# Moving every large SBUF tile of an attention and two-layer MLP kernel to a multiple of 2 KB

## The chip, the cores and the metric

The kernel runs on one core of a Trainium2 chip. Its engines are named as the profile names them: PE is the matrix engine (PEld its weight loads), DVE the vector engine, ACT the scalar engine, POOL the GpSimd engine, SP the engine whose queue issues the DMAs. The metric is the device time of one execution in microseconds (us). On-chip memory here means SBUF: 128 partitions, and each tile has the same byte address in all of them.

## What is computed

```python
# attention: 2 x 8 heads, 768 positions, head size 64
scores = q @ k.T / 8 + bias          # bias = -slope(head) * distance
a = softmax(where(keep, scores, -1e9))   # keep: 8 global keys and the 96 last ones
x = (a @ v).reshape(1536, 512)
# layer 1, d_ff 2048
h = x @ w_in;  x = softplus(h) @ w_out
# layer 2, d_ff 2048
h = x @ w_in;  x = (h * clip(h + 3, 0, 6) / 6) @ w_out
```

## The kernel before

`body` (L763) opens one pool of small constants, `const`, and calls `fast_path` (L411). `fast_path` opens the pool `xp` with the transposed activations (`xsh`, `xsl`: the high and the low part of x, three tiles each of 8 KB a partition) and builds `Layers` (L52), which opens `mp` (the split activations `gh` and `gl`), `tp` (scratch `t`), `pp` (three 8 KB tiles `part` of partial sums, and the one-column constant `three` that the second layer's ACT instruction at L182 adds), `wp0` (six slots of four 2 KB weight tiles `w`) and `wr0` (raw weights and their scratch `wa`). After these `fast_path` opens the pools of attention: `ap_r`, `ap2` (`qT`), `ap_v` (`V`), `ap_m` (`pm` and the row statistics), `ap_t` (`pT`) and `ap1` (`kT`, `gk`, `zeros`, `bias`). When attention is over, its pools close and `wp1` and `wr1` take their place: five more slots of weights.

A bump allocator lays the pools one behind the other in the order in which they are opened; a tile takes its size, rounded up to 32 bytes. No table says where a tile begins: it is the sum of all that was opened earlier.

Every product of the layers is written as three products of float32r parts (high by low, low by high, high by high; `matmul3`, L188), all issued at L193. Each of them is one LDWEIGHTS of 128 columns and one MATMUL. The moving operand is streamed through the array, the stationary one is loaded ahead of it. Which tile is which differs by stage:

| stage | output | moving operand (columns) | stationary operand (128 columns) |
|---|---|---|---|
| first layer, first phase, beside attention | `hf`, `accf` | `xsh`/`xsl`, `gh`/`gl` (256) | `w` |
| first layer, rest | `h`, `acc` | `xsh`/`xsl`, `gh`/`gl` (512) | `w` |
| second layer | `h`, `acc` | `xsh`/`xsl` for `h`, `w` for `acc` (512) | `w` for `h`, `gh`/`gl` for `acc` |
| closing stage (`last_items`, L302) | `hz`, `accz` | `xsh`/`xsl` for `hz`, `w` for `accz` (512, the last block in halves of 256) | `w` for `hz`, `g` for `accz` |

The closing stage keeps its `gh` and `gl` for all five chunks at once, so `last_items` puts them not into `mp` but into free weight slots of `wp0` and `wp1` (`where`, L316, tiles named `g`). Everything else about `accz` is as in the second layer's `acc`.

The raw weights are float64, read as pairs of 32-bit words, and are turned into the two float32r parts of `w` on the chip (`unit_convert`, L117: ACT L133 and L145, POOL L136, DVE L137, L140, L141, L146), one or two units beside each item of matmuls. While attention runs, the first raw tiles and scratch tiles are parts of `part` instead of `wr0`. In the last phases `check_step` (L611) reads q and k once more, squares them on ACT (L624) and sets a flag that decides whether a second, general path is run; with these inputs it is not.

The engines each take their instructions in the order written out at build time by a scheduler; waits are on semaphores.

Of the kernel before, what the change touches and what calls it, by code (L numbers as in the profile page):

```python
# [7 lines left out]
F32 = mybir.dt.float32  # L8
# [8 lines left out]
P = 128  # L17
# [20 lines left out]
BIG = float(2 ** 38)  # L38
FAR = 1.0e9
SCALE = 0.125  # L40
EPS = 1e-9
SQ_LIMIT = 1.0e9
W_LO = 2.0 ** -15
# [8 lines left out]
class Layers:  # L52
# [3 lines left out]

    def __init__(self, ctx, tc, weights, xsh, xsl, out):
        self.ctx, self.tc, self.nc = ctx, tc, tc.nc  # L60
        self.weights, self.xsh, self.xsl, self.out = weights, xsh, xsl, out
        self.pool("mp", 2)
        self.pool("tp", 5)
        self.pool("pp", 1)
        self.part = [self.pp.tile([P, 4, GB], F32, name=f"part{g}") for g in range(T // GB)]
        self.three = self.pp.tile([P, 1], F32, name="three")
        self.nc.vector.memset(self.three, 3.0)
        self.W, self.raws, self.slot = {}, {}, {}
        self.done, self.loaded = 0, 0
        first = range(PHASES[0][0])  # L70
        early = range(2 * EARLY_PAIRS)
        self.order = [(j, u) for js in (early, first[len(early):]) for u in range(2) for j in js]
        self.order += [(j, u) for j in range(len(first), 2 * NCH) for u in range(2)]
        self.free, self.h_tags, self.acc_tags, self.wr = [], [], [], []
        self.room = None
        self.n_h, self.halves, self.in_first, self.beside = 0, 0, True, False
        self.grow(0, FIRST_SLOTS, 2, 2)
# [318 lines left out]
def x_tiles(ctx, tc):  # L396
    xp = ctx.enter_context(tc.tile_pool(name="xp", bufs=1))
    return tuple(
        [xp.tile([P, KC, GB], F32R, name=f"xs{z}{g}") for g in range(T // GB)] for z in "hl"
    )  # L400


def softmax_rows(nc, sm, rs, pm):

    nc.vector.tensor_scalar(out=rs, in0=sm, scalar1=EPS, scalar2=None, op0=ALU.add)
    nc.vector.reciprocal(out=rs, in_=rs)  # L406
# [1 line left out]
        nc.gpsimd.tensor_scalar(out=t, in0=t, scalar1=rs[:, j:j + 1], scalar2=0.0, op0=ALU.mult, op1=ALU.add)  # L408


def fast_path(tc, ident, nf, counts, q, k, qt, kt, v, weights, out, flag):  # L411


    with ExitStack() as ctx, ExitStack() as actx:
        nc = tc.nc
        xsh, xsl = x_tiles(ctx, tc)
        layers = Layers(ctx, tc, weights, xsh, xsl, out)
        layers.beside = True
        tp = layers.tp
        layers.room = actx.enter_context(tc.tile_pool(name="ap_r", bufs=1))  # L420
# [52 lines left out]
        for h in range(H):  # L473
            nc.scalar.mul(bias[:, h, 2, :], far[:, 2, :], -SLOPES[h] / SCALE)

        def bias_of(hs):
            for h in hs:
                tc.keep_in_program_order(nc.vector.tensor_scalar(
                    out=bias[:, h, 0:2, :], in0=far[:, 0:2, :], scalar1=-SLOPES[h] / SCALE, scalar2=None, op0=ALU.mult
                ))  # L480
# [6 lines left out]
        def att_s(k):  # L487
# [28 lines left out]
            for z in range(4):  # L516
# [3 lines left out]
                    in1=bias[:, 4 * e + z, mo:mo + nsl, :].rearrange("p s t -> p (s t)"),  # L520
                    scale=-SCALE, scalar=3.0e38, op0=ALU.add, op1=ALU.min, accum_out=nm[:, z:z + 1],
                )
# [138 lines left out]
def dense_attention(tc, ident, nf, q, k, v, xsh, xsl):  # L661

    with ExitStack() as ctx:
# [25 lines left out]
        for i in range(NB):  # L689
# [20 lines left out]
            for b in range(B):  # L710
                for c in range(KC):
# [8 lines left out]
                    for j in range(2):  # L720
# [4 lines left out]
                        for z in range(2):  # L725
# [3 lines left out]
                            )  # L729
                            nc.scalar.mul(pm[:, z * S // 2:(z + 1) * S // 2], ps[:, z, 0:S // 2], SCALE)  # L730
                        nc.vector.scalar_tensor_tensor(
# [19 lines left out]
                    nc.vector.tensor_tensor(out=xl, in0=px, in1=r32(xh), op=ALU.subtract)  # L751


def general_path(tc, ident, nf, q, k, v, weights, out):
    with ExitStack() as ctx:
        xsh, xsl = x_tiles(ctx, tc)
        dense_attention(tc, ident, nf, q, k, v, xsh, xsl)
        layers = Layers(ctx, tc, weights, xsh, xsl, out)
        layers.weight_step(2 * FIRST_SLOTS)
        layers.run()  # L760


def body(tc, q, k, v, qt, kt, ns, w1i, w1o, w2i, w2o, out):  # L763
    nc = tc.nc
    with ExitStack() as ctx:
        nc.scalar.preload_act_table_set("natural_log_exp_and_others")
        const = ctx.enter_context(tc.tile_pool(name="const", bufs=1))
        ident = const.tile([P, P], F32, name="ident")

        nsb = const.tile([P, 2, 2], I32, name="nsb")  # L770
        nc.sync.dma_start(out=nsb.rearrange("p n w -> p (n w)"), in_=ns.partition_broadcast(P))
        nf = const.tile([P, 2], F32, name="nf")
        cv = const.tile([P, 2, 2], F32, name="cv")
        cneg = const.tile([P, 2], F32, name="cneg")

        def counts():
            tc.keep_in_program_order(nc.vector.tensor_copy(cv, nsb))
            nc.vector.tensor_scalar(out=cneg, in0=cv[:, :, 0], scalar1=0.0, scalar2=None, op0=ALU.is_lt)
            nc.vector.tensor_tensor(out=cneg, in0=cneg, in1=cv[:, :, 1], op=ALU.add)
            nc.vector.scalar_tensor_tensor(  # L780
                out=nf, in0=cneg, scalar=float(2 ** 32), in1=cv[:, :, 0], op0=ALU.mult, op1=ALU.add
            )

        make_identity(nc, ident)
        flag = const.tile([1, 1], I32, name="flag")
        weights = (w1i, w1o, w2i, w2o)
        fast_path(tc, ident, nf, counts, q, k, qt, kt, v, weights, out, flag)
        redo = nc.values_load(flag[0:1, 0:1], min_val=0, max_val=1)
        with tc.If(redo > 0):
            general_path(tc, ident, nf, q, k, v, weights, out)  # L790


def layout(q, k, v, n_global, n_local, moe_w_in, moe_w_out, moe2_w_in, moe2_w_out):
# [43 lines left out]
```

## Time and profile before

| | us |
|---|---|
| median of 3 runs (range) | 643.96 (643.88 to 644.82) |
| the profiled execution | 643.55 |
| its span, first to last instruction | 641.8 |
| PE busy in it | 622.3 |
| DVE busy | 425.7 |
| ACT busy | 380.8 |
| POOL busy | 148.1 |

The profiled execution is 0.41 us under the median, and 1.75 us of it lie outside the span. Busy time of PE counts a matmul from its start to a modelled end, so that neighbours overlap; what a matmul costs in a stream is the step from one start to the next. The chain that ended last goes back from the last instruction to what released each one; where PE works without a gap, a piece of it is a number of matmuls and the time that they took together, which gives the step.

### The profile page before, as it was taken

To read this page: it belongs to the slowest core of one execution; us is meant where nothing else is said; L and a number is where in the kernel's file an instruction comes from. 1 tells how busy PE (TensorE), PEld (TensorE's weight loads), DVE (VectorE), ACT (ScalarE), POOL (GpSimd) and SP (SyncE) were. 2 spreads that over 40 slices of the span, in tenths; PEclk is the share of its full clock that TensorE was granted. 3 is DMA by queue.
4 is the path that set the end of the run, shared out by engine and by line. 5 is a ranking of instruction groups with operands and counts; after the bars stand their busy time and mean duration, and the time that the engine had idled before them with its cause. 6 is when DMAs were issued, how large, how long until landed. Compare 5 with 4: busy or idle time off the path is not lost.

```text
span 641.8 us, 9651 instructions
## 1 busy us (share of the span) xinstructions
PE 622.3 (97%) x3496; PEld 513.1 (80%) x3496; DVE 425.7 (66%) x893; ACT 380.8 (59%) x808; POOL 148.1 (23%) x180
## 2 busy tenths in 40 slices
PE   8699999999999999999999999999999999999996
PEld 4477987899999888887888888888887888888785
DVE  6988687735799999999989994126723342424251
ACT  7978888764868877696777652326694222222230
POOL 4666354330133255352200600001000000000000
PEclk9989999999999999999999999999999999999999
DMA  8754231101233333433402132001562000001011
GB/s 279 247 172 137 72 100 38 42 5 66 73 126 133 130 115 118 131 130 100 132 1 66 66 106 91 0 1 33 164 197 67 0 1 0 2 1 65 1 67 70
DMA packets 25081, 53.67 MB, mean 84 GB/s; under 512 B 2496, under 2 KB 9152, under 8 KB 25024
## 3 DMA queue, kind: packets, MB, share of 16 engines
q1 hardware_dynamic: 25024, 52.96, 25.4%
q8 instruction: 29, 0.48, 0.3%
q14 instruction: 28, 0.23, 0.1%
HBM read 49.81 MB, written 3.15 MB: 83 GB/s over the span
## 4 chain that ended last, share of the span: by engine, by line
PE 62%; DVE 17%; ACT 9%; DMA 5%; issue 3%; POOL 3%; SPq 0%; ACTq 0%; POOLq 0%; DVEq 0%
PE acc L193 21%; PE h L193 21%; PE accf L193 6%; PE hf L193 5%; ACT pm L523 3%; DVE wa L140 2%; DMA chk<-in_q 2%; PE accz L193 2%; PE hz L193 2%; DVE wa L141 2%; DVE w L146 2%; PE ptp L546 2%; POOL wa L136 1%; ACT chk L624 1%; PE px L564 1%
## 5 line engine op out<-in xcount | busy, mean ns | idle before, releaser
L193 PE MATMUL h<-xsh,w 128*128 128x512 f32 x584 | 159.1, 396 | 0.0
L136 POOL TENSOR_SCALAR wa<-wa 128x512 f32<-128x512 f32 x56 | 79.4, 1423 | 235.4 <-ACT wa L133 235.2
L193 PEld LDWEIGHTS h<-xsh,w 128*128 128x128 f32 x584 | 109.3, 188 | 26.7 <-DVE t L179 0.7
L193 PE MATMUL acc<-w,gh 128*128 128x512 f32 x344 | 108.0, 395 | 0.0
L183 DVE SCALAR_TENSOR_TENSOR t<-t,h 128x512 f32<-128x512 f32 x43 | 29.4, 684 | 82.3 <-ACT t L182 82.3
L193 PE MATMUL h<-xsl,w 128*128 128x512 f32 x292 | 82.3, 395 | 0.0
L182 ACT ACTIVATE t<-h,three 128x512 f32<-128x512 f32 x43 | 29.5, 687 | 87.7 <-PE h L193 87.5
L185 DVE TENSOR_TENSOR gl<-t,gh 128x512 fp32r<-128x512 f32 x73 | 51.3, 703 | 42.9 <-ACT gh L184 42.6
L193 PE MATMUL acc<-gh,w 128*128 128x512 f32 x240 | 78.9, 396 | 0.3 <-DVE part L289 0.2
L193 PEld LDWEIGHTS acc<-w,gh 128*128 128x128 f32 x344 | 64.5, 188 | 15.7
L184 ACT CAST gh<-t 128x512 fp32r<-128x512 f32 x73 | 45.2, 619 | 46.3 <-PE acc L193 24.3
L193 PE MATMUL acc<-w,gl 128*128 128x512 f32 x172 | 68.2, 396 | 0.1
L408 POOL TENSOR_SCALAR pm<-pm,rs 128x256 f32<-128x256 f32 (+1 forms) x96 | 54.4, 585 | 58.9 <-DVE rs L406 34.2
L193 PEld LDWEIGHTS h<-xsl,w 128*128 128x128 f32 x292 | 54.8, 188 | 13.2
L193 PE MATMUL accf<-ghf,w 128*128 128x256 f32 x288 | 56.6, 286 | 0.2 <-ACT ghf L184 0.2
L193 PEld LDWEIGHTS acc<-gh,w 128*128 128x128 f32 x240 | 44.9, 188 | 11.9 <-DVE part L289 0.6
L523 ACT ACTIVATE pm<-pm,nm 128x256 f32<-128x256 f32 (+1 forms) x96 | 46.3, 485 | 3.3 <-DVE nm L518 3.1
L193 PE MATMUL acc<-gl,w 128*128 128x512 f32 x120 | 47.5, 396 | 0.0
L193 PE MATMUL hf<-xsh,w 128*128 128x256 f32 x288 | 47.2, 289 | 0.0
L193 PEld LDWEIGHTS accf<-ghf,w 128*128 128x128 f32 x288 | 45.9, 188 | 0.6 <-ACT ghf L184 0.4
L146 DVE TENSOR_TENSOR w<-wa,w 128x512 fp32r<-128x512 f32 x56 | 39.4, 705 | 8.9 <-ACT w L145 8.9
L145 ACT CAST w<-wa 128x512 fp32r<-128x512 f32 x56 | 34.3, 615 | 14.4 <-DVE wa L141 8.9
(115 smaller groups left out, 1045.9 us busy)
## 6 DMA issues: line engine op xcount, KB each, us to landing
raw<-in_w2i SPq DMA_DIRECT2D x16, 512.0 KB, 3.3
raw<-in_w2o SPq DMA_DIRECT2D x16, 512.0 KB, 3.3
raw<-in_w1i SPq DMA_DIRECT2D x14, 512.0 KB, 3.4
raw<-in_w1o SPq DMA_DIRECT2D x12, 512.0 KB, 3.3
V<-in_v SPq DMA_DIRECT2D x12, 256.0 KB, 3.0
chk<-in_q SPq DMA_DIRECT2D x12, 256.0 KB, 3.0
chk<-in_k SPq DMA_DIRECT2D x12, 256.0 KB, 2.8
qT<-in_qt SPq DMA_DIRECT2D x11, 256.0 KB, 3.9
```

Of the source, the lines that this page charges most:

```text
L136: nc.gpsimd.tensor_scalar(out=a, in0=a, scalar1=W_HI, scalar2=W_LO, op0=ALU.min, op1=ALU.max)
L140: nc.vector.scalar_tensor_tensor(out=ai, in0=hi, scalar=-2 ** 30, in1=ai, op0=ALU.bitwise_and, op1=ALU.bitwise_or)
L141: nc.vector.scalar_tensor_tensor(out=ai, in0=lo, scalar=29, in1=ai, op0=ALU.logical_shift_right, op1=ALU.bitwise_or)
L145: nc.scalar.copy(wh, a)
L146: nc.vector.tensor_tensor(out=wl, in0=a, in1=r32(wh), op=ALU.subtract)
L182: nc.scalar.activation(t1, hf, AF.Relu, bias=self.three[:, 0:1])
L183: nc.vector.scalar_tensor_tensor(out=t3, in0=t1, scalar=6.0, in1=hf, op0=ALU.min, op1=ALU.mult)
L184: nc.scalar.copy(gh, t3)
L185: nc.vector.tensor_tensor(out=gl, in0=t3, in1=r32(gh), op=ALU.subtract)
L193: return self.nc.tensor.matmul(out, lhsT=a, rhs=b, start=start and z == 0, stop=stop and z == len(seq) - 1, **kw)
L408: nc.gpsimd.tensor_scalar(out=t, in0=t, scalar1=rs[:, j:j + 1], scalar2=0.0, op0=ALU.mult, op1=ALU.add)
L523: nc.scalar.activation(pmz, pmz, AF.Exp, bias=nm[:, z:z + 1], scale=-1.0, accum_out=sm[:, z:z + 1])
```

## The change

The constant `three` moves from `pp` into `const`, and takes 1,248 bytes there (312 float32 columns, of which the first is used) instead of 32. Its memset is now issued in `body`; it stays the first instruction of DVE. In the path that runs, the order of all instructions on all engines, their shapes and their waits are those of before; what differs is the addresses.

```diff
+EDGE = 312
...
-    def __init__(self, ctx, tc, weights, xsh, xsl, out):
+    def __init__(self, ctx, tc, weights, three, xsh, xsl, out):
...
-        self.three = self.pp.tile([P, 1], F32, name="three")
-        self.nc.vector.memset(self.three, 3.0)
+        self.three = three
...
         make_identity(nc, ident)
         flag = const.tile([1, 1], I32, name="flag")
+        three = const.tile([P, EDGE], F32, name="three")[:, 0:1]
+        nc.vector.memset(three, 3.0)
```

Where the tiles begin, as the built programs have it (first byte of the pool, and in brackets what it is past a multiple of 2,048):

| pool | tiles | before | after |
|---|---|---|---|
| `xp` | `xsh`, `xsl` | 17,184 (800) | 18,432 (0) |
| `mp` | `gh`, `gl` | 66,336 (800) | 67,584 (0) |
| `tp` | `t`, `rel`, `far` and the like | 74,528 (800) | 75,776 (0) |
| `pp` | `part` | 84,768 (800) | 86,016 (0) |
| `wp0` | `w`, and `g` in the closing stage | 109,376 (832) | 110,592 (0) |
| `wr0` | `raw`, `wa` | 158,528 (832) | 159,744 (0) |
| `ap_r`, `ap2`, `ap_v`, `ap_m` | raw, `qT`, `V`, `pm` | 170,816 (832) | 172,032 (0) |
| `ap_t` | `pT` | 203,968 (1,216) | 205,184 (384) |
| `ap1` | `kT`, then `gk`, `zeros`, `bias` | 212,160 (1,216) | 213,376 (384) |
| `wp1` | `w`, and `g` in the closing stage | 170,816 (832) | 172,032 (0) |
| `wr1` | `raw`, `wa` | 211,776 (832) | 212,992 (0) |

The row statistics in `ap_m` (12 tiles of 32 bytes) stand ahead of `ap_t`, so `pT`, `kT` and what follows begin 384 bytes past. Before, the pools up to `pp` stood 32 bytes off those behind it, because of the 32 bytes of `three`; after, both groups stand at the same offset. The identity used by the transposes stays at 16,512 (128).

## Rows read from the trace of the kernel before

**Rows 1.** Page, the span and the busy time by engine.
```profile
span 641.8 us, 9651 instructions
...
PE 622.3 (97%) x3496; PEld 513.1 (80%) x3496; DVE 425.7 (66%) x893; ACT 380.8 (59%) x808; POOL 148.1 (23%) x180
```
**Rows 2.** Chain that ended last, shares of the span by engine, then by line.
```profile
PE 62%; DVE 17%; ACT 9%; DMA 5%; issue 3%; POOL 3%; SPq 0%; ACTq 0%; POOLq 0%; DVEq 0%
by line: PE acc L193 21.5%; PE h L193 20.7%; PE accf L193 6.3%; PE hf L193 5.3%; ACT pm L523 2.9%; issue 2.8%; DVE wa L140 2.2%; DMA chk<-in_q 2.2%; PE accz L193 2.2%; PE hz L193 2.2%; DVE wa L141 2.1%; DVE w L146 1.8%; PE ptp L546 1.8%; PO
```
**Rows 3.** Chain in order of time, second layer: start us, us, what.
```profile
508.76 2.80 PE acc L193 x12
511.56 2.80 PE h L193 x12
514.36 2.80 PE acc L193 x12
```
**Rows 4.** The same, end of the first layer's first phase.
```profile
168.74 2.84 PE hf L193 x24
171.59 2.84 PE accf L193 x24
174.42 2.84 PE hf L193 x24
```
**Rows 5.** The same, the closing stage.
```profile
612.17 9.32 PE hz L193 x40
621.49 12.03 PE accz L193 x60
```
**Rows 6.** The same, asked for 623 to 630 us alone.
```profile
622.88 7.25 PE accz L193 x32
```
**Rows 7.** Timeline of PE, the last block's halves: start us, us, operation, names.
```profile
631.67 1.72 PE L193 MATMUL accz<-w,g 128*128 128x256 f32 x13
```
**Rows 8.** PE by line and shape: busy us, mean ns of one, idle before.
```profile
L193 PE MATMUL accf<-glf,w 128*128 128x256 f32 x144 | 40.5, 282 | 0.9 <-DVE glf L185 0.9
L193 PE MATMUL hf<-xsl,w 128*128 128x256 f32 x144 | 22.9, 281 | 0.0
```
**Rows 9.** Windows: busy us of PE, PEld, DVE, ACT, POOL, PEclk, DMA share, GB/s.
```profile
211.00:301.00 90.00, 89.82 (x385) 71.81 (x383) 89.49 (x154) 66.86 (x117) 39.81 (x22) 1.00 0.37 122
441.00:490.00 49.00, 49.00 (x211) 39.31 (x210) 25.63 (x42) 34.42 (x83) 3.48 (x5) 1.00 0.51 151
505.00:525.00 20.00, 20.00 (x88) 16.07 (x87) 4.83 (x7) 4.68 (x8) 0.00 (x0) 1.00 0.00 1
623.00:630.00 7.00, 7.00 (x33) 5.79 (x32) 0.98 (x3) 0.62 (x1) 0.00 (x0) 1.00 0.01 2
```
**Rows 10.** Chain in order of time, around 301 and 490 us.
```profile
300.78 0.63 ACT gh L184
301.41 0.04 issue
301.45 0.73 PE acc L193 x2
...
486.08 2.59 DMA chk<-in_k
...
489.48 0.52 ACT gh L184
490.00 0.02 issue
490.02 0.70 DVE gl L185
```
**Rows 11.** One line each of ACT and DVE: ns min/median/max, first and last start.
```profile
L145 ACT CAST w<-wa x56: 602/613/627, 35.4 to 471.1; 128x512 fp32r<-128x512 f32 x56
L145 ACT CAST w<-part x8: 614/625/653, 21.5 to 91.1; 128x512 fp32r<-128x512 f32 x8
...
L146 DVE TENSOR_TENSOR w<-wa,w x56: 673/680/1080, 37.2 to 471.7; 128x512 fp32r<-128x512 f32 x56
L146 DVE TENSOR_TENSOR w<-part,w x8: 654/680/944, 22.8 to 92.3; 128x512 fp32r<-128x512 f32 x8
```
**Rows 12.** DMA issues: KB each, median us from issue to landing.
```profile
chk<-in_q SPq DMA_DIRECT2D x12, 256.0 KB, 3.0
chk<-in_k SPq DMA_DIRECT2D x12, 256.0 KB, 2.8
```
**Rows 13.** The memset of `three`: ns min/median/max, first and last start.
```profile
L67 DVE MEMSET three<- x1: 59/59/59, 0.8 to 0.8; 128x1 f32 x1
```
**Rows 14.** Timeline of PE, the second warm-up on tile `zeros`, bf16.
```profile
9.44 1.47 PE L647 MATMUL warm<-zeros 128*128 128x512 bf16 x6
```
**Rows 15.** The warm-up's line: ns min/median/max, first and last start.
```profile
L647 PE MATMUL warm<-zeros x24: 379/384/634, 1.2 to 17.6; 128*128 128x512 bf16 x24
```

More of the change, by code (lines that the diff above doesn't have):

```diff
@@ L408, in softmax_rows, with fast_path @@
         nc.gpsimd.tensor_scalar(out=t, in0=t, scalar1=rs[:, j:j + 1], scalar2=0.0, op0=ALU.mult, op1=ALU.add)
-def fast_path(tc, ident, nf, counts, q, k, qt, kt, v, weights, out, flag):
+def fast_path(tc, ident, three, nf, counts, q, k, qt, kt, v, weights, out, flag):
     with ExitStack() as ctx, ExitStack() as actx:
@@ L416, in fast_path @@
         xsh, xsl = x_tiles(ctx, tc)
-        layers = Layers(ctx, tc, weights, xsh, xsl, out)
+        layers = Layers(ctx, tc, weights, three, xsh, xsl, out)
         layers.beside = True
@@ L751, in dense_attention, with general_path @@
                     nc.vector.tensor_tensor(out=xl, in0=px, in1=r32(xh), op=ALU.subtract)
-def general_path(tc, ident, nf, q, k, v, weights, out):
+def general_path(tc, ident, three, nf, q, k, v, weights, out):
     with ExitStack() as ctx:
@@ L757, in general_path @@
         dense_attention(tc, ident, nf, q, k, v, xsh, xsl)
-        layers = Layers(ctx, tc, weights, xsh, xsl, out)
+        layers = Layers(ctx, tc, weights, three, xsh, xsl, out)
         layers.weight_step(2 * FIRST_SLOTS)
@@ L785, in body @@
         flag = const.tile([1, 1], I32, name="flag")
+        three = const.tile([P, EDGE], F32, name="three")[:, 0:1]
+        nc.vector.memset(three, 3.0)
         weights = (w1i, w1o, w2i, w2o)
-        fast_path(tc, ident, nf, counts, q, k, qt, kt, v, weights, out, flag)
+        fast_path(tc, ident, three, nf, counts, q, k, qt, kt, v, weights, out, flag)
         redo = nc.values_load(flag[0:1, 0:1], min_val=0, max_val=1)
         with tc.If(redo > 0):
-            general_path(tc, ident, nf, q, k, v, weights, out)
+            general_path(tc, ident, three, nf, q, k, v, weights, out)
 def layout(q, k, v, n_global, n_local, moe_w_in, moe_w_out, moe2_w_in, moe2_w_out):
```

## The prediction

> **What bounds the kernel now.** I read the busy times first, then the chain that ended last, then single stretches of that chain. PE is busy in 97% of the span and no other engine in more than 66% [rows 1]. The chain shows where that matters: 62% of it lies on PE, the rest on DVE, ACT, DMA and POOL, and its largest pieces are the matmuls of L193: `acc` 21.5%, `h` 20.7%, `accf` 6.3%, `hf` 5.3%, `accz` and `hz` 2.2% each [rows 2]. The change leaves every instruction as it was and moves operands, so the question is whether the step from one matmul to the next depends on where its operands lie. Such a dependence would show as different steps for equal shapes.
>
> They differ. In the second layer 12 matmuls of 512 columns take 2.80 us, both for `acc` and for `h`: a step of 233.3 ns [rows 3]. In the first phase, 24 of 256 columns take 2.84 us: 118.3 ns [rows 4]. In the closing stage `hz` still has 9.32 / 40 = 233.0 ns, and `accz`, right behind it, is quicker: 12.03 us for 60, of which 15 have half the columns [rows 5]. The part of it without halves and without its first matmuls has 7.25 / 32 = 226.6 ns [rows 6]. So the same shape has two steps, 6.7 ns apart. The halves of the last block go the other way: 13 of them end 1.72 us after the first starts; less the modelled length of one, some 0.28 us [rows 8], that is 1.44 / 12 = 120.0 ns [rows 7], 1.7 ns more than a 256-column matmul has elsewhere.
>
> What sets `accz` apart? [...] Not the shape or the order of products, which are those of `acc`. By the table of addresses it is this: everywhere else in the layers one operand begins 800 bytes past a multiple of 2 KB (`xp` or `mp`) and the other, a weight tile, 832; in `accz` both are weight slots, at 832. A difference of 32 bytes between the operands, or one operand off a multiple of 64 bytes, goes with 233.3 ns; equal offsets on multiples of 64 go with 226.6 ns. Whether the odd operand is the moving one (`h`) or the stationary one (`acc` of the second layer) makes no difference [rows 3]. Straddling a 2 KB boundary is not it: `hf` at 168.74 us reads x from byte 800 of a 2 KB row on, `hf` at 174.42 us from 1,824 on and over the boundary, and both take 2.84 us [rows 4]. After the change every operand of L193 begins at a multiple of 512 bytes, and all are alike.
>
> **The change, part by part.** *Matmuls of 512 columns.* `acc`, `h` and `hz` hold 21.5 + 20.7 + 2.2 = 44.4% of the chain [rows 2], 285 us of 641.8, or 1,221 steps of 233.3 ns. At 226.6 ns each saves 6.7 ns: 8.2 us off the path.
>
> *Matmuls of 256 columns.* `accf` and `hf` hold 11.6%, 74.4 us or 629 steps of 118.3 ns. At the 120.0 ns of the closing halves they cost 1.1 us more. I take this in full, since it is the only row with equal offsets; the other end is nothing.
>
> *Stretches where PE is not the chain.* From 211 to 301 us DVE is busy 89.49 of 90 us, and from 441 to 490 the chain runs through the reloads of q and k and their squares on ACT; PE works 385 and 211 matmuls there [rows 9]. A shorter step gains nothing in them: PE comes to the same `gh` and `gl` earlier and waits. At 301.45 it starts 0.04 us behind the ACT cast of `gh`, at 490 it waits for `gl`, queued on DVE behind a cast that stood behind a square on ACT, which waited for its DMA [rows 10]. What is late next is thus known: 385 x 6.7 ns = 2.6 us of new idle time on PE before 301 us, 211 x 6.7 ns = 1.4 us before 490. If those engines yielded it after all, 4.0 us more would be gained; if PE followed DVE up to 345 us, some 189 more steps or 1.3 us would be lost.
>
> *ACT and DVE.* The weight cast on ACT takes 613 ns from `wa` (832 to 832) and 625 ns from `part` (800 to 832); the DVE difference behind it takes 680 ns in both cases [rows 11]. DVE gains nothing by this; on ACT 12 of 625 ns of its 9% (58 us) [rows 2] would be at most 1.1 us. I take 0, as nearly all of ACT's work has one offset already.
>
> *DMA.* It holds 5% of the chain, 32 us [rows 2]. No row shows a landing on a 2 KB multiple; the reloads of q and of k, equal in size and place, differ by 0.2 of 3.0 us [rows 12], so I allow 7% either way, 2.2 us, and take 0. [...]
>
> *The constant.* The memset takes 59 ns at 0.8 us [rows 13] and stays DVE's first instruction: 0.
>
> The sum is -8.2 + 1.1 = -7.1 us. The profiled execution has 643.55 us, 0.41 less than the median; off that median, 643.96, it gives 636.9 us. Its own range is 632 (the 4.0 us yielded and something of ACT or DMA) to 640.4 (1.3 and 2.2 us lost).
>
> **The rivals.** *Addresses do not matter.* Then `accz` is quicker for a reason that I do not see, for instance because only there do both operands lie above byte 109,376. For it: its first six matmuls are slower than the rest (12.03 us less 15 x 0.12 and 39 x 0.2266 leaves 1.39 us, 232 ns each [rows 5]), although their operands lie at 832 as well. Against it: no matmul of 512 columns outside it shows the short step in the rows I read, at any distance of the operands. Time: 644.0, or 645.1 if the 256-column matmuls alone take their 120.0 ns. [...]
>
> *Equal places collide: slower.* The moving tile and the first slice of the weights would now begin at the same place of a 2 KB row in nearly every matmul, on a multiple that no row shows, and the loading of the next weights beside the stream could hold the stream up. The halves at 120.0 against 118.3 ns [rows 4, 7] show that equal offsets can cost. Priced at as large a step the other way, 6.7 ns on 1,221 matmuls and 1.1 us on the short ones: 653.3 us. It decides as soon as the step of `h` passes 234.4 ns (1.3 us over 1,221).
>
> *Finer alignment gives more.* 832 is a multiple of 64 and of no larger power of two, so `accz` may not be the best. The bf16 warm-up has six matmuls of 512 columns in 1.47 us [rows 14], less the length of one, 0.38 [rows 15]: 218 ns. At that step 1,221 x 15.3 ns = 18.7 us would go: 625.3 us. Nothing shows that float32r reaches it.
>
> **How the numbers follow.** A measurement of this kernel can tell about 0.2%, 1.3 us, from no change. The forecast gets 0.58: the contrast is clean, but rests on one stage and its cause on a table. No effect gets 0.22, slower 0.12, more gain 0.08. Faster by over 0.2%: the forecast and the larger gain less a little for a gain eaten by waits, 0.64; within: 0.22; slower: 0.14, with the case of 645.1. The range runs from the forecast's low end, 632, to the no-effect case with its 1.1 us, 645.1; outside are the larger gain and most of the collision, under 0.2.
>
> **What would show it.** Right: 12 `h` or `acc` in 2.72 us instead of 2.80, `hz` at the step of `accz`, `hf` and `accf` 24 in 2.88, `accz` unchanged, PE idle some 2.6 us before 301 us and a chain there on DVE as now. Wrong: `h` still 2.80 per 12 (addresses do not matter), over 2.81 (collision), or near 2.62 (finer alignment). If the step falls and the time does not, the gain sits as idle time on PE in front of `gh` and `gl`.

## The result, and the profile after

| | before | after |
|---|---|---|
| median of 4 runs (range), us | 643.98 (643.88 to 644.82) | 636.26 (635.85 to 637.12) |
| ratio to before, 95% interval | | 0.987 (0.986 to 0.989) |
| the profiled execution, us | 643.55 | 637.12 |

The change made the kernel 7.7 us faster; 636.9 had been predicted, in a range of 632.0 to 645.1. The profiled execution of after is the longest of its four, 0.86 us over the median, so the trace shows 6.4 us of the 7.7.

The page, span and busy times by engine:

```profile
span 635.3 us, 9650 instructions
...
PE 615.2 (97%) x3495; PEld 515.3 (81%) x3496; DVE 426.6 (67%) x893; ACT 380.7 (60%) x808; POOL 139.8 (22%) x180
```

The same work as in [rows 1]: PE still has 97% of the span, and the span and PE's busy time fell together, by 6.5 and 7.1 us.

The chain in order of time (start us, us, what), in the first phase, around 302 us, in the second layer and in the closing stage:

```profile
168.82 2.88 PE hf L193 x24
171.70 2.88 PE accf L193 x24
...
301.81 0.63 ACT gh L184
302.44 0.04 issue
302.49 1.20 PE acc L193 x4
...
508.06 2.72 PE h L193 x12
510.78 2.72 PE acc L193 x12
...
605.88 9.07 PE hz L193 x40
614.95 12.00 PE accz L193 x60
```

Twelve `h` or `acc` take 2.72 us, 226.7 ns each, where they took 2.80 [rows 3]; 24 `hf` or `accf` take 2.88, 120.0 ns each, where they took 2.84 [rows 4]; 40 `hz` take 9.07 instead of 9.32 [rows 5]. `accz` has 12.00 for 60 against 12.03: it already had the short step. At 302.49 PE still starts 0.04 us behind the ACT cast of `gh`, as at 301.45 before [rows 10].

Where along the program the gain comes shows in the first and last start of each kind of matmul. PE by operation, before (count, ns min/median/max, first and last start in us):

```profile
L193 PE MATMUL acc<-gh,w x240: 388/395/499, 208.2 to 376.4; 128*128 128x512 f32 x120
...
L193 PE MATMUL accz<-w,g x75: 277/389/397, 621.3 to 635.8; 128*128 128x512 f32 x45, 128*128 128x256 f32 x30
```

And after:

```profile
L193 PE MATMUL acc<-gh,w x240: 388/389/499, 208.4 to 375.3; 128*128 128x512 f32 x120
...
L193 PE MATMUL accz<-w,g x75: 278/389/390, 614.8 to 629.2; 128*128 128x512 f32 x45, 128*128 128x256 f32 x30
```

The first phase ends 0.2 us later. From there to the end of the first layer's `acc` 168.2 us became 166.9, from there to the first `accz` 244.9 became 239.5, and from `accz` to the end of the span it is 20.5 in both. So in this trace 5.4 of the 6.5 us come from the second layer with its 1,092 matmuls of 512 columns, and only 1.3 from the rest of the first layer with 720.

Windows after (busy us of PE, PEld, DVE, ACT, POOL, PEclk, DMA share, GB/s):

```profile
211.00:301.00 90.00, 87.60 (x381) 70.81 (x380) 89.49 (x153) 67.05 (x116) 36.05 (x22) 1.00 0.36 118
441.00:490.00 49.00, 48.14 (x211) 38.86 (x210) 25.90 (x41) 34.92 (x82) 3.01 (x4) 1.00 0.47 140
505.00:525.00 20.00, 20.00 (x90) 16.58 (x89) 7.39 (x11) 4.34 (x7) 0.00 (x0) 1.00 0.00 1
```

Against [rows 9]: from 211 to 301 us DVE is as busy as before (89.49), PE does 381 matmuls instead of 385 and now stands idle 2.40 us; from 441 to 490 it does the same 211 and is idle 0.86 us. Where nothing holds it, at 505 to 525 us, with POOL and the DMA share at 0.00 before and after, it does 90 instead of 88.

What the prediction had put at nothing, after (DMA issues: KB each, median us to landing; then lines of ACT and DVE):

```profile
chk<-in_q SPq DMA_DIRECT2D x12, 256.0 KB, 3.4
chk<-in_k SPq DMA_DIRECT2D x12, 256.0 KB, 2.7
...
L145 ACT CAST w<-wa x56: 600/616/627, 35.0 to 467.5; 128x512 fp32r<-128x512 f32 x56
L145 ACT CAST w<-part x8: 612/620/646, 21.3 to 90.9; 128x512 fp32r<-128x512 f32 x8
...
L146 DVE TENSOR_TENSOR w<-wa,w x56: 672/680/1078, 37.0 to 468.2; 128x512 fp32r<-128x512 f32 x56
```

The reload of q lands 0.4 us later and that of k 0.1 us earlier than in [rows 12]; the cast from `wa` has 616 ns for 613, the one from `part` 620 for 625, and the DVE difference 680 as before [rows 11].

### The profile page after: what moved, and what is told of

It is laid out like the page before. It is cut to its first block, busy times and chain, and to the rows that moved or that the text cites. A ratio compares the mean times of both kernels' runs of the same rounds, so it can differ in the third digit from the quotient of the medians.

```text
span 635.3 us, 9650 instructions
## 1 busy us (share of the span) xinstructions
PE 615.2 (97%) x3495; PEld 515.3 (81%) x3496; DVE 426.6 (67%) x893; ACT 380.7 (60%) x808; POOL 139.8 (22%) x180
## 3 DMA queue, kind: packets, MB, share of 16 engines
HBM read 49.81 MB, written 3.15 MB: 83 GB/s over the span
## 4 chain that ended last, share of the span: by engine, by line
PE 64%; DVE 15%; ACT 9%; DMA 5%; issue 3%; POOL 3%; SPq 0%; ACTq 0%; POOLq 0%; DVEq 0%
PE acc L193 21%; PE h L193 20%; PE accf L193 6%; PE hf L193 5%; ACT pm L523 3%; PE ptp L546 2%; DVE wa L140 2%; DMA chk<-in_q 2%; PE accz L193 2%; PE hz L193 2%; DVE wa L141 2%; DVE w L146 2%; PE px L564 2%; PE s L512 2%; POOL wa L136 1%
## 5 line engine op out<-in xcount | busy, mean ns | idle before, releaser
L193 PE MATMUL h<-xsh,w 128*128 128x512 f32 x584 | 155.8, 390 | 1.7 <-DVE t L179 1.7
L136 POOL TENSOR_SCALAR wa<-wa 128x512 f32<-128x512 f32 x56 | 71.3, 1278 | 240.3 <-ACT wa L133 240.0
L193 PE MATMUL acc<-w,gh 128*128 128x512 f32 x344 | 106.0, 389 | 0.0
L193 PE MATMUL h<-xsl,w 128*128 128x512 f32 x292 | 80.5, 389 | 0.0
L133 ACT ACTIVATE wa<-raw 128x512 f32<-128x512 f32 x53 | 35.6, 675 | 14.4 <-DVE w L146 7.0
```

What stands on the lines that cost most here:

```text
L133: first = nc.scalar.activation(a, raw.bitcast(F32)[:, :, 1], AF.Abs)
L136: nc.gpsimd.tensor_scalar(out=a, in0=a, scalar1=W_HI, scalar2=W_LO, op0=ALU.min, op1=ALU.max)
L193: return self.nc.tensor.matmul(out, lhsT=a, rhs=b, start=start and z == 0, stop=stop and z == len(seq) - 1, **kw)
```

## The experiments

The theory that came out of the result: what counts is where the two operands of a matmul lie relative to each other. Its rivals: a multiple of 64 bytes or of 2 KB counts for each tile alone; the absolute place counts; DMA, DVE or ACT gained by the new places.

**Everything equal, at other places.** Only the width of the constant changes, so all pools of the layers stand at one offset: 832 bytes past 2 KB (a multiple of 64), then 32 past (a multiple of no more than 32).

```diff
-EDGE = 312
+EDGE = 8      # all832
+EDGE = 320    # all32
```

> Every operand at 832 past a multiple of 2 KB (a multiple of 64, not of 128): the constant takes 32 bytes in the constants' pool instead of 1,248. If a multiple of 64 bytes and equal offsets are enough: the kernel after, 636.3 us within 0.2%, 12 h in 2.72 us. If the multiple of 2 KB itself does it: 644.0 us, 12 h in 2.80 us, only accz short.

> Every operand at 32 past a multiple of 2 KB: equal offsets, all of them off a multiple of 64. If equal offsets of the two operands do it: 636.3 us, 12 h in 2.72 us. If each operand has to begin on a multiple of 64: 12 h in 2.80 us or more and 644 us, and if each operand off it costs a share of its own, 12 h in 2.88 us and about 652 us.

Measured: 636.75 us at 832 (ratio 0.988, 0.986 to 0.990) and 635.84 at 32 (0.988, 0.986 to 0.990), both the changed kernel's time within their intervals. The chain of the kernel at 32, in order of time:

```profile
163.49 2.88 PE hf L193 x24
...
506.89 2.72 PE h L193 x12
...
604.71 9.07 PE hz L193 x40
```

The same steps as after. Neither 2 KB nor 64 bytes is needed. As weights, raw tiles and reloads lie at 832 or 32 here and the whole gain is there, none of it came from DMA, DVE or ACT at the new places, as far as runs can tell that agree within some 1.3 us.

**The weights moved off by 32 and by 64 bytes.** The changed kernel, with x and `gh` still on multiples of 2 KB and a small unused tile in `pp`, which shifts `wp0` and all behind it.

```diff
+        self.pad = self.pp.tile([P, 8], F32, name="pad")    # w32
+        self.pad = self.pp.tile([P, 16], F32, name="pad")   # w64
```

> x, gh/gl and the sums at 0, weights and all behind them at 32: the 32 bytes between the two groups are back. If the offset between the operands is the cause: 12 h in 2.80 us, 24 hf in 2.84 us and 644.0 us within 0.2%; accz (both operands at 32) tells the two theories apart, 7.25 us for 32 if equal offsets do it, longer if a multiple of 64 is needed. If the cause is the place of the tiles in memory as such, or their multiple of 2 KB: between 636 and 644 us.

> x, gh/gl and the sums at 0, weights and all behind them at 64: both on multiples of 64, 64 bytes apart. If a multiple of 64 for each is enough: 636.3 us, 12 h in 2.72 us. If equal offsets in a longer line (128 bytes or more) are needed: 12 h in 2.80 us or between, up to 644 us.

Measured with 32: 644.08 us, ratio 1.000 (0.999 to 1.001): the whole gain is gone. Its chain:

```profile
163.26 2.84 PE hf L194 x24
...
509.70 2.80 PE acc L194 x12
...
613.11 9.32 PE hz L194 x40
622.43 12.03 PE accz L194 x60
```

Every piece is that of before, although x lies as in the changed kernel. `accz`, whose two operands both lie at 32 here, has its 12.03 us of before too, and so the short step: equal places are enough for it, and a multiple of 64 is not needed. With 64: 640.98 us, 0.996 (0.994 to 0.997). Its chain:

```profile
164.99 2.72 PE accf L194 x24
167.71 2.72 PE hf L194 x24
...
506.10 2.76 PE acc L194 x12
508.86 2.80 PE h L194 x12
```

Now the 512-column `h` has the long step, 233.3 ns, the second layer's `acc` 230.0 (there the weights are the moving operand, so the stationary one stands 64 bytes before it and not behind it), and the 256-column matmuls are quicker than in any kernel so far: 113.3 ns. (Over the whole phase their mean step, from start to start, is 113.7 to 115.0.) Of the three distances tried so far, 0 is the best for 512 columns and the worst for 256, and a multiple of 64 on both sides does not help `h`.

**The distance by itself.** A kernel without attention and layers: streams of 24 matmuls on two tiles, 512 and 256 columns in turn, the stationary operand d bytes past the moving one, d from 0 to 496 in steps of 16, the whole of it from byte 0 of the tiles and again from byte 32. A second kernel walks through slices in the order of the real one, in steps of 4 bytes.

```diff
+for base in (0, 8):
+    for d in list(range(0, 512, 16)) + [4, 8, 0]:
+        for cols in (512, 256):
...
+                    acc[:, 0:cols], lhsT=sta[:, base + d // 4:base + d // 4 + P],
+                    rhs=mov[:, base:base + cols], start=z == 0, stop=z == 23,
```

> Computes none of the reference: only streams of 24 matmuls, 512 and then 256 columns, one moving and one stationary tile, the stationary one starting d bytes further than the moving one (d = 0, 16, ... 496, then 4, 8 and 0 again), all of it once from byte 0 and once from byte 32 of the tiles. If the offset between the operands sets the step: d = 0 has 226.7 ns (512 columns) and 120.0 (256), d = 32 has 233.3 and 118.3, d = 64 has 233.3 and 114, as in the kernels, and the run from byte 32 repeats that from byte 0. If the step also needs the neighbours of the real kernel (DVE, ACT, DMA), all d are alike. If only multiples of 64 count, d = 64, 128, ... have the step of d = 0.

> Computes none of the reference: as the sweep before, but with the operands in the order of the kernel's h (four slices of the moving tiles 2 KB apart, four of the stationary tiles 512 bytes apart, high and low parts in turn), and the stationary tiles d = 0, 4, 8, ... 252 bytes further than the moving ones. If the offset within 256 bytes sets the step whatever slice is read: the steps of the sweep at each d that both have (226.7 and 120.0 ns at 0, 233.4 and 118.5 at 32, 233.5 and 117.7 at 64, 226.7 at 144), and at 64 not the 114 ns that 256 columns had in the kernel. If the order of slices counts too: 114 at 64, and other values elsewhere. An offset with a shorter step than 226.7 for 512 columns would make a quicker kernel.

The first kernel's chain, with d at 32, 64, 144 and 256 bytes, then 0 from byte 0 (`dcq`, right behind streams at d = 8) and from byte 32 on (`dcs`, behind d = 0); all have 512 columns but `daj`, which has 256, at d = 64:

```profile
23.81 5.60 PE dae L785 x24
...
40.69 5.59 PE dai L785 x24
46.28 2.83 PE daj L785 x24
...
82.88 5.45 PE das L785 x24
...
141.52 5.45 PE dbg L785 x24
...
292.74 5.49 PE dcq L785 x24
...
301.10 5.45 PE dcs L785 x24
```

At 512 columns 24 took 5.45 us, 227 ns each, at d = 0 (`dcs`), 144 and 256, and 5.49 to 5.61, 229 to 234 ns, at the other multiples of 16 up to 240. But for the kernel's first stream, each piece comes back 256 bytes further to within 0.01 us; starting from byte 32 changes none by more. The short step is not always there at once: `dcq` took 5.49 us, 0.04 more than `dcs`, although its operands stand at distance 0 from its first matmul on; `dbg`, right behind a stream at d = 240, took 5.45. The kernel with the real order of slices, at d = 64 (`dbg` with 512 columns, `dbh` with 256), 100 (`dby`), 144 (`dcu`) and 156 (`dda`):

```profile
145.78 5.59 PE dbg L789 x24
151.38 2.73 PE dbh L789 x24
...
221.48 5.45 PE dby L789 x24
...
314.04 5.60 PE dcu L789 x24
...
339.31 5.84 PE dda L789 x24
```

Here d = 144 has the long step (233.3 ns), d = 156 one of 243 ns, longer than any behind the first stream of the first kernel, d = 100 the short one (227 ns), and d = 64 gives a mean of 113.8 ns at 256 columns, where the first kernel had 117.9. So the order in which slices follow each other counts beside the distance, and the first loop's table of distances did not hold in the second. No stream of 512 columns, at any of the 64 distances or in the first kernel, took less than 5.45 us for 24, 227 ns.

**Does DVE hold part of the gain back?** The kernels of before and after with one DVE instruction of the weights' conversion left out, the one that puts in the low word.

```diff
-        nc.vector.scalar_tensor_tensor(
-            out=ai, in0=lo, scalar=29, in1=ai, op0=ALU.logical_shift_right, op1=ALU.bitwise_or
-        )
```

> The kernel before without the third DVE instruction of each weight unit's conversion (the low word is left out of the weights), 64 of 0.68 us: DVE is relieved where it holds the chain before 301 us. Faster than before by some us; only its distance to the next kernel counts.

> The kernel after without the same instruction. If the part of the gain that is missing before 301 us is held by DVE: the distance to the kernel before so relieved is 9.5 to 10.5 us instead of 7.7, and PE has under 1 us of idle time between 211 and 300 us. If PE's own steps make up all of the gain and nothing is held back: 7.7 us again.

Measured: 641.42 and 629.80 us, a distance of 11.6 instead of 7.7, and 1.1 more than the upper end expected. Windows of the lighter before:

```profile
211.00:301.00 90.00, 90.00 (x387) 72.55 (x386) 85.75 (x143) 69.96 (x121) 18.66 (x21) 1.00 0.40 130
...
441.00:490.00 49.00, 49.00 (x212) 39.44 (x211) 22.62 (x37) 34.98 (x82) 2.84 (x4) 1.00 0.48 140
```

And of the lighter after:

```profile
211.00:301.00 90.00, 90.00 (x398) 74.51 (x397) 85.79 (x146) 71.80 (x126) 22.59 (x21) 1.00 0.41 139
...
441.00:490.00 49.00, 49.00 (x218) 40.58 (x217) 21.34 (x35) 32.42 (x76) 1.57 (x2) 1.00 0.47 135
```

With DVE relieved, 85.8 of 90 us instead of 89.49, PE works without a gap in both stretches, and the short step shows as 11 and 6 more matmuls in them. By the prediction's own terms that is its 8.2 us and the 4.0 us that it kept out of the sum, less 1.1: 11.1, against 11.6 by the medians. The first stretch is DVE's, as expected. In the second DVE was never at its limit (25.9 of 49 us in the changed kernel), so why the gap there goes as well is not shown.

**A kernel that takes the best of both.** Each stage gets its own distance: the weights of the first phase's six chunks begin 64 bytes past x, all others are equal, both up to multiples of 256 bytes. Two weight tiles of 2 KB become one of 4 KB, with 256 spare bytes in `wp0` and none in `wp1`, and a chunk's slices begin 64 bytes later or not. To make room the constant has 32 bytes, so that x and `gh` lie at 832; in the last kernel it has 224, and they lie at 1,024.

```diff
+SHIFT = 16
...
+            o = SHIFT if j < PHASES[0][0] else 0
+            for i in range(2):
+                pair = wp.tile([P, 2 * CW + self.spare(t)], F32R, tag=f"w{i}_{t}", name=f"w{i}_{j}")
+                self.W[j] += [pair[:, o:o + CW], pair[:, o + CW:o + 2 * CW]]
...
-EDGE = 312
+EDGE = 8     # both, light_both
+EDGE = 56    # both_1k
```

> The weights of the first layer's first phase (six chunks) begin 64 bytes past a multiple of 256 relative to x, gh and gl; every other weight tile, and the tiles g of the closing stage, begin at the same offset as their partner (all at 832 past 2 KB, the changed kernel's relation at another place). Theory of the distance between the operands: hf and accf go from 119.8 to the 113.3 to 115 ns seen in the experiment with weights at 64, all else keeps 226.7. About 630 steps of 256 columns lie on the chain; at 6.0 ns each 3.8 us go: 632.5 us, ratio 0.982, if no other engine holds the phase. Rival: the phase's gain is held by ACT and DVE, which make softmax tiles, gh and weights there, or is given back as new idle time of PE before 301 us: 635 us or more, ratio 0.986 or above, with the steps at 113 to 115 all the same.

> The changed kernel itself, once more, as the companion of the kernel with weights at 64 in the first phase: ratio 0.987, steps 226.7 and 119.8.

> The kernel with weights at 64 bytes in the first phase, with the third DVE instruction of the weights' conversion (the one that puts in the low word) left out, as in the two lighter kernels before. If DVE is what holds the first phase's gain back, this one stands 3.5 to 4 us under the lighter changed kernel's 629.8 us: 626 us, and more than the distance between the kernel with 64 bytes and the changed one in full. If the phase is held by ACT or by attention itself, the distance is the same small one in both, under 2 us.

> The kernel with weights at 64 bytes in the first phase, with the constant widened by 192 bytes, so that x, gh, gl begin on a multiple of 256 (1,024 past 2 KB) instead of 64 past one; every distance between operands stays as in that kernel. There hf and accf came to 115.4 to 116.4 ns, not the 113.7 to 115.0 of the experiment with all weights at 64, where x lay at 0. If the absolute place makes the 2 ns, the steps go to 113.7 to 115.0 and some 630 x 1.5 = 1 us is gained: 633.5 us, ratio 0.983. If the place is without effect, as in the two halves of the sweep, the steps stay at 116.3 and the time at 634.6, ratio 0.985; then it is the distances of 320, 576 and on, which the 256 bytes between the weight tiles bring, or the order of the slices.

| kernel | us, median | ratio to before (95%) | 256-column step, mean ns |
|---|---|---|---|
| the changed kernel again | 636.57 | 0.988 (0.986 to 0.990) | 119.6 to 119.9 |
| 64 bytes in the first phase, x at 832 | 634.61 | 0.985 (0.983 to 0.986) | 115.4 to 116.4 |
| the same, x at 1,024 | 632.88 | 0.983 (0.982 to 0.984) | 113.6 to 115.1 |
| the lighter one, x at 832 | 627.68 | 0.974 (0.972 to 0.976) | 115.4 to 116.4 |

The kernel with 64 bytes and x at 832 gained 2.0 us on the changed one and not the 3.8 expected, but neither theory put down ahead of it was right about why. The lighter pair has about the same distance (629.80 to 627.68, 2.1 us), which speaks against DVE holding the phase, though the two intervals touch; the step itself came out at some 116 ns, and 629 steps by 3.5 ns are 2.2 us. Moving x and `gh` from 832 to 1,024, from 64 past a multiple of 256 to 0, with every distance kept, brought the step down to a mean of some 114.5 ns. That is worth about 1 us; the medians differ by 1.7, but their intervals overlap, so the step shows the effect and the time alone does not. The chain of that kernel, first phase and second layer:

```profile
151.80 2.72 PE hf L201 x24
154.52 2.72 PE accf L201 x24
...
505.35 2.72 PE h L201 x12
508.07 2.72 PE acc L201 x12
```

These pieces are all at their best at once, 113.3 ns and 226.7 ns, and the time, 632.88 us, is the lowest of the kernels that compute the weights in full, with an interval that lies apart from the changed kernel's.

The second trace of the changed kernel, taken for this table, has a span of 634.5 us, 0.8 less than the first. It says how far single readings of the first one hold:

```profile
L193 PE MATMUL acc<-gh,w x240: 388/389/504, 209.4 to 375.9; 128*128 128x512 f32 x120
...
L193 PE MATMUL accz<-w,g x75: 277/389/390, 614.3 to 628.7; 128*128 128x512 f32 x45, 128*128 128x256 f32 x30
...
211.00:301.00 90.00, 87.89 (x383) 71.23 (x382) 89.49 (x154) 67.80 (x118) 36.67 (x22) 1.00 0.36 119
441.00:490.00 49.00, 48.77 (x215) 39.81 (x214) 26.18 (x42) 35.03 (x82) 3.01 (x4) 1.00 0.47 145
```

The steps are the same, and so is DVE's hold from 211 to 301 us (2.11 us idle). But the first phase ends 1.2 us later than before and not 0.2, the first layer's rest gains 1.7 us and the second layer 6.5, and from 441 to 490 us PE is idle 0.23 us instead of 0.86.

## Why the prediction was right

*The cause.* The reading of the two steps of one shape, with the table of addresses beside it, was right: operands that stand 32 bytes apart have 233.3 ns, equal ones 226.7. The prediction left open whether it is "a difference of 32 bytes between the operands, or one operand off a multiple of 64 bytes". The kernels at 32 everywhere (off 64, short step) and at 64 for the weights alone (on 64, long step for `h`) settle it for the difference. The prediction's remark that `accz` has the order of products of `acc` holds only for the three parts of a product (`accz` goes through five chunks for one slice, `acc` through four slices for one chunk); with every distance equal both have 226.7 ns, so this did not set them apart. The 2 KB of the change's title play no part; 32 bytes of a constant, moved from one pool to another, do.

*The terms.* Both steps came out as named: 2.72 us for 12, 2.88 for 24, `hz` at the step of `accz`. The 1.1 us of the 256-column matmuls, taken in full, show at the end of the first phase as 0.2 us in one trace of the changed kernel and 1.2 in the other, and as 0.6 and 0.8 in the kernels with all at 32 and at 832, with the same steps in all four. The kernel with weights at 32 ends the phase 0.2 later as well, with the steps of before. So the step of the term is right (means of 119.8 ns for 118.2), and whether part of it is hidden beside attention is not shown.

*What PE can't use.* Of 2.6 us of new idle time before 301 us 2.2 came (0.18 before, 2.40 after), and 1.9 in the second trace; the lighter pair showed that this is DVE's hold. Of 1.4 before 490, 0.9 came in the first trace and 0.2 in the second, so there the prediction's claim that a shorter step gains nothing holds in part only: the chain waits for reloads there, and from 440 to 500 us those of q hold 14.5 us of it in the first trace and held 14.1 before. The start behind `gh` at 301.45 is at 302.49 in the first trace: the prediction had named a loss of up to 1.3 us there if PE follows DVE, and had it at nothing in the sum. Of the 1.04, 0.2 were already there at the end of the first phase, so some 0.8 was lost.

*The sum.* In the first trace, then, the 256-column term came out 0.9 us smaller than said and the rest of the first layer gained 0.9 less than the 2.2 us of its 335 steps outside the stretch before 301 us. That these two cancel is luck. The second layer gave 5.4 of the 5.9 us of its 881 steps outside the stretch before 490 us. So the profiled executions stand 6.4 us apart and the medians 7.7, for the 7.1 predicted. The size of the step and the number of steps are not luck; they are read from rows and came back in every kernel with equal places.

*DMA, ACT, DVE at nothing.* Right within the noise: the reload of q landed later and that of k earlier, the casts moved by 3 to 5 ns either way, and the gain is the same with all tiles at 832 (636.75 us, no slower than 636.26 beyond the noise). The later landing of q is no clear effect of the addresses either: single landings of q spread further than that in one and the same kernel, the four in the chain from 3.14 to 3.97 us before and from 3.15 to 3.88 after.

*The rivals.* That addresses don't matter fell with the kernel whose weights alone lie 32 bytes off, 644.08 us: its `acc` has 233.3 ns where the changed kernel's has 226.7, and the two kernels differ by the address alone. The few slower matmuls at the start of `accz`, which spoke for that rival, are gone: 60 now take 12.00 us, which is 45 x 0.2267 + 15 x 0.120. They belong to the stage ahead and not to the place of `accz`: they are there again, with the same 12.03 us, in the kernel with weights at 32, where `hz` ahead of them has the long step, and not in the kernels where `hz` has the short one; the sweep's `dcq`, behind streams at another distance, is 0.04 us longer than `dcs` too. The collision would have needed more than 234.4 ns, and the step went down. Finer alignment giving more fell too: no stream of 512 columns in either sweep is under 227 ns, so the 218 of the bf16 warm-up was not to be had by any distance tried in these streams.

## What to carry to other kernels

When one shape of matmul has two steps in a trace, lay the table of operand addresses beside it before looking for waits; here the 32 bytes of a small tile in an early pool set them for nearly the whole kernel, 233.3 ns or 226.7. Make the distance between moving and stationary operand what the long stage wants (0 bytes here), and give a stage with another number of columns its own distance (64 here, 113.3 ns for 120.0), but measure it in that loop with its own order of slices: at 64, 24 of 256 columns took 2.83 us in one sweep and 2.73 in the other. Before 301 us, where DVE was busy for 89.49 of 90 us, the shorter step ended as idle time of PE, 2.2 us of 2.6, and could be left out of the sum; before 490 us, where the chain waits for reloads of q that take 3.14 to 3.97 us, 0.9 us of 1.4 came in one trace and 0.2 in the other, so part of it may be gained. Take a second trace before a difference of under 1 us is read from one.

## What the runs showed of the hardware

- With float32r operands the step of a stream depended on the distance between its two operands. At 512 columns it was 226.7 ns at 0 and 233.3 at 32 in the kernels, 227 to 234 in the plain sweep, with a period of 256 bytes, and up to 243 (at 156) in the sweep with the real order of slices; at 256 columns it went from 113.3 (weights at 64) to 123 (at 204, real order), with 120 at 0. What in the chip does it was not found.
- Behind a stream at another distance the step is not always reached at once: `dcq` took 5.49 us for 24 and `dcs` 5.45, and the first five steps of `accz` before had 228 to 236 ns, the next ones 226 to 227; `dbg`, behind d = 240, had its 5.45.
- The best distance for one width was not that of the other: 0 bytes gave the shortest step at 512 columns, 226.7 ns, and one of the longest at 256, 120.0 against 113.3 at 64.
- The absolute place did nothing at distance 0 (0, 32 and 832 past 2 KB: 226.7 and 119.8 ns) but something at 64: with x 64 past a multiple of 256 the mean 256-column step was some 116 ns, on the multiple 114.5. One place of each kind was tried, so which multiple counts is open. The plain sweep, which started only at 0 and 32, had not shown it.
